# Attention into a token and channel mixer on one core: five small moves in the start-up, and a third output tile

## The chip, the cores and the metric

The kernel runs on one core of a Trainium2 chip. The metric is the device time of one execution in microseconds (us). Three runs of the kernel before gave 394.48, 394.86 and 395.20 us, with a median of 394.86 us.

The engines are named as in the profile: PE is the matrix engine (PEld its weight loads), DVE the vector engine, ACT the scalar engine, POOL the GpSimd engine, SP the engine that only issues transfers here. A line number such as L301 is a line of the kernel before.

## What is computed

Cosine attention over 8 batches, 12 heads, 448 positions and 64 elements per head, and behind it a mixer over tokens and channels:

```python
q_n = q / (norm(q) + 1e-06);  k_n = k / (norm(k) + 1e-06)      # over the 64 elements
attn = softmax(q_n @ k_n.T / tau)                               # tau = 0.1
x = (attn @ v), heads side by side                              # 8 x 448 x 768
h = relu(x.T @ w_tok1) @ w_tok2                                 # 448 -> 256 -> 448, over tokens
u = x + h.T
out = u + relu(u @ w_ch1) @ w_ch2                               # 768 -> 1536 -> 768, over channels
```

Inputs, weights and output are 32-bit floats.

## The kernel before, in words

**Units of work.** Two heads of one batch make a pair; there are 48 pairs, six to a batch, and three pairs make a "half" (half 0 is pairs 0 to 2, half 1 is pairs 3 to 5, and so on). A sequence of 448 positions is held as three chunks of 128 ("main") and a rest of 64 ("x" in the names: `xq`, `xk`, `xv`, `sqx`).

**What a pair goes through.** Squares of q and k (`squares`, `squares_x`, line 178 on ACT, line 180 on DVE or POOL), their sums by DVE (`sums`, `sums_x`, lines 193 and 197), reciprocal norms by four short ACT operations (`rnorms`, lines 201 to 204), scaling of k and q by these norms (`scaled` line 211, `scaled_x` lines 217 and 222, mostly POOL), transposes on PE into the PSUM tile `pst` (`tpose`, lines 243 to 248), a DVE copy of it to `qk` (`qk_copy`, line 261), three main score products into `psS` and their exponentials on ACT (`score`, lines 301 and 302), one product for the rest (`score_x`, lines 308 and 309), the product with the values into `psO` (`pv`, lines 320 and 322), and the division on DVE (`rec` line 326, `x` line 327). From pair 15 on the transposes are done by the DMA engines instead.

**The mixer.** `m_tok1` multiplies by `w1t` into `psR` (line 341) and DVE takes the positive part to `r` (line 344). `m_tok2` multiplies by `w2t` into `psU` (line 361), adds x through the identity (line 366), and DVE casts the sum to `ut` (line 368). Six pairs complete a batch; then `m_ch1` (`psG`, lines 389 and 391) and `m_ch2` (`psF`, line 404) do the channel part, in units that are fed in between the steps of later pairs. The result is added to the transposed u by DVE into an output tile `ost` (line 407), which a DMA on SP's queue sends out (lines 414 to 417). Each `ost` tile is filled by two such additions; the pool `outp` holds two tiles.

**Order of the work.** The order on every engine is that of the program text; nothing reorders it. After a start-up written out by hand, a loop over slots i = 0 to 49 issues the steps; tables such as `sq_at`, `sum_at`, `rn_at`, `sc_at` and `cast_at` say in which slot a pair's squares, sums, norms, scaling and value casts stand. Each engine works through its own list in order, and waits at the head of it. PSUM tiles come from two rings: `ps2` with three places for `psS`, `psX`, `psO` and `psR`, and `ps` with two for `pst`, `psG`, `psF` and (for the first two batches) `psU`.

**What the change and the steps below touch.**
- `weights_tok` (lines 140 to 144) issues three DMAs on POOL's queue, which convert from 32 to 16 bits on the way: the main part of `w1t`, its rest of 64 rows, and `w2n`, the second token weight as it lies in memory. It stands in the start-up behind `score_x(0)`.
- `place_w2` (lines 147 and 149) and `place_w2_odd` (line 152) copy `w2n` on DVE into the order that `m_tok2` wants: `w2t` has columns XR to S for the main positions, and the 64 rest positions both behind them (line 149, columns S to S+64) and ahead of them (line 152, columns 0 to 64), since even batches read columns 64 to 512 and odd ones 0 to 448. `place_w2` stands at the end of slot 2, `place_w2_odd` at the end of slot 3.
- `cast_v` (line 166) casts a half's values to `vt`; for half 1 it stands in slot 3, ahead of the `m_tok2` of pair 0. `cast_vx` (line 172, POOL) does the rest rows.
- The squares of pair 3 and those of the rest rows of half 1 stand in slot 0, both q and k on ACT.

Of the kernel before, what the change touches and what calls it, by code (L numbers as in the profile page):

```python
# [22 lines left out]
def kernel(  # L23
# [12 lines left out]
    nc = tc.nc  # L36

    B, H, S, E = q.shape
# [5 lines left out]
    NC = 3  # L44
    SM = P * NC
# [93 lines left out]

    def weights_tok():  # L140
        nc.gpsimd.dma_start(out=w1t[:, 0:NC, :], in_=moe_w_tok1[0:SM].rearrange("(p c) t -> p c t", c=NC))
        nc.gpsimd.dma_start(out=w1t[0:XR, NC, :], in_=moe_w_tok1[SM:S])
        w2n.append(mix.tile([P, TT, S], FP16, name="w2n", tag="gt16", bufs=1))
        nc.gpsimd.dma_start(out=w2n[0][:], in_=moe_w_tok2.rearrange("(tt p) s -> p tt s", p=P))

    def place_w2():
        nc.vector.tensor_copy(out=w2t[:, :, XR:S].rearrange("t a (c p) -> t a c p", c=NC),
                              in_=w2n[0][:, :, 0:SM].rearrange("t a (p c) -> t a c p", c=NC))
        nc.vector.tensor_copy(out=w2t[:, :, S:S + XR], in_=w2n[0][:, :, SM:S])  # L149

    def place_w2_odd():
        nc.vector.tensor_copy(out=w2t[:, :, 0:XR], in_=w2n[0][:, :, SM:S])

# [301 lines left out]
    early_sq = {3: 0, 4: 1, 5: 1, 6: 3, 7: 4, 8: 5, 9: 5, 10: 6, 11: 7, 12: 8, 13: 9, 14: 9, 15: 10, 16: 11, 17: 11}  # L455
    sq_slot = {p: early_sq.get(p, p - 6) for p in range(3, NP_ALL)}
    sq_at = at(sq_slot)
    sum_at = at({p: s + 1 for p, s in sq_slot.items() if p < 8 or p >= 18})

    rn_at = {}  # L460
    for n in range(1, NHALF):
        for c0, c1 in ((0, 21), (21, 45)) if n < 4 else ((0, 45),):
            s = 1 + sq_slot[3 * n + (0 if c1 == 21 else 2)]
            rn_at.setdefault(s, []).append((n, c0, c1))
# [47 lines left out]
    with tc.manual_schedule():  # L512
# [75 lines left out]
        score_x(0)  # L588
        weights_tok()
        cast_vx(0)  # L590
        cast_v(0)
        scaled(2, nc.gpsimd)
        for i in range(NP_ALL + 2):
# [30 lines left out]
            def next_sq(ps):  # L624
                for p in ps:
                    norm_begin(p, nc.scalar if p < 18 else nc.gpsimd, nc.scalar if p == 3 else nc.vector if p in (10, 11, 12, 15) else nc.gpsimd)

# [144 lines left out]
```

## Time and profile before

| | |
|---|---|
| three runs | 394.48, 394.86, 395.20 us |
| the profiled execution | 394.72 us |
| its span, first to last instruction | 392.9 us |
| PE busy | 378.7 us (96%) |
| ACT, POOL, DVE busy | 225.8, 209.6, 193.5 us |
| bytes moved by DMA | 67.51 MB, 172 GB/s in the mean |

Where PE was busy, by stretches of the span (us):

| stretch | length | PE busy |
|---|---|---|
| 0 to 10 | 10 | 8.39 |
| 10 to 30 (slots 0 to 3) | 20 | 14.32 |
| 30 to 45 | 15 | 13.35 |
| 45 to 90 | 45 | 44.31 |
| 90 to 100 | 10 | 8.79 |
| 100 to 380 | 280 | 279.86 |
| 380 to 392.9 | 12.9 | 9.70 |

Engine rows of the timeline read "start, length, engine, line, operation, output <- inputs, shapes, count", and in brackets the idle time ahead of it with what ended it. A length includes the tail of an operation, which overlaps the next one; the spacing of the starts is the time that an operation costs its engine when several stand in a row. The list of waits reads "who waited <- for whom: total us, times, longest us". The chain of waits follows the last instruction back through whatever released each step, and reads "start, length, engine, line".

### The profile page before, as it was taken

How to read it: one execution, taken by the hardware profiler on the slowest of the kernel's cores; microseconds unless marked ns; L12 is line 12 of the kernel's file. 1: busy time of each engine (PE TensorE's matmuls, PEld its weight loads, DVE VectorE, ACT ScalarE, POOL GpSimd, SP SyncE). 2: the span in 40 equal slices, each digit the busy share in tenths (PEclk: the TensorE clock that was granted, in tenths of full speed). 3: DMA queues.
4: the chain of work that ended last, by engine and by line, in shares of the span. 5: the costliest groups of instructions: out<-in, count | busy, mean ns of one | idle time of the engine just before them, and what ended most of it. 6: DMA issues, size and time to landing. Idle time of an engine off the chain costs nothing.

```text
span 392.9 us, 9076 instructions
## 1 busy us (share of the span) xinstructions
PE 378.7 (96%) x3658; PEld 228.5 (58%) x3658; DVE 193.5 (49%) x368; ACT 225.8 (57%) x411; POOL 209.6 (53%) x306
## 2 busy tenths in 40 slices
PE   8678999998999999999999999999999999999996
PEld 3346555665565656566556566566566566565554
DVE  5688758865344554545524645345534342333022
ACT  5998698843774639573676446673775536511400
POOL 4978486789267584868572947659561700000000
PEclk9899999999999999999999999999999999999999
DMA  7999999969968987999989899999982452013013
GB/s 203 276 238 253 246 236 215 227 138 264 209 131 190 202 183 179 222 183 208 205 199 198 175 245 216 166 189 182 242 142 56 123 123 68 16 57 102 5 40 120
DMA packets 137514, 67.51 MB, mean 172 GB/s; under 512 B 93248, under 2 KB 134016, under 8 KB 137472
## 3 DMA queue, kind: packets, MB, share of 16 engines
q1 hardware_dynamic: 133296, 61.36, 71.4%
q0 software_dynamic: 3632, 5.18, 7.4%
q8 instruction: 28, 0.46, 0.5%
q10 hardware_dynamic: 544, 0.39, 0.3%
q14 instruction: 14, 0.11, 0.1%
HBM read 43.38 MB, written 11.01 MB: 138 GB/s over the span
## 4 chain that ended last, share of the span: by engine, by line
PE 86%; ACT 6%; DVE 3%; DMA 2%; SPq 1%; issue 1%; ACTq 0%; DVEq 0%
PE psF L404 28%; PE psG L389 27%; PE psO L320 9%; PE psS L301 7%; PE psR L341 5%; PE psU L361 4%; ACT pt L302 3%; PE psO L322 3%; PE psX L308 2%; DMA out_dram<-ost 1%; DMA km<-in_k_dram 1%; PE psU L366 1%; PE pst L243 1%; ACT sq L178 1%; DVE ost L407 1%
## 5 line engine op out<-in xcount | busy, mean ns | idle before, releaser
L302 ACT ACTIVATE pt<-psS 128x896 f16<-128x896 f32 x141 | 119.0, 921 | 65.8 <-PE psS L301 65.5
L389 PE MATMUL psG<-ut,wc1t 128*128 128x448 f16 x576 | 119.5, 353 | 0.2
L404 PE MATMUL psF<-wc2t,gt 128*128 128x384 f16 (+2 forms) x684 | 117.3, 324 | 1.2 <-DVE ost L407 1.1
L391 ACT ACTIVATE gt<-psG 128x448 f16<-128x448 f32 x96 | 51.1, 557 | 73.2 <-PE psG L389 73.2
L404 PEld LDWEIGHTS <-gt 128*128 128x128 f16 x684 | 64.5, 98 | 48.4 <-issue 8.1
L389 PEld LDWEIGHTS <-wc1t 128*128 128x128 f16 x576 | 53.2, 98 | 52.5 <-issue 8.7
L211 POOL TENSOR_TENSOR kq<-km,rn 128x384 f16<-128x384 f32 x47 | 39.4, 837 | 80.9 <-ACT rn L204 80.7
L407 DVE TENSOR_TENSOR ost<-psF,ur 128x384 f32<-128x384 f32 (+2 forms) x57 | 31.4, 550 | 90.0 <-PE psF L404 86.6
L320 PEld LDWEIGHTS <-pt 128*128 128x128 f16 x1152 | 50.1, 97 | 8.4 <-issue 2.4
L320 PE MATMUL psO<-vt,pt 128*128 128x65 f16 x1152 | 52.4, 193 | 1.2 <-ACT pt L302 0.8
L326 DVE RECIPROCAL rec<-psO 128x8 f32<-128x8 f32 x48 | 9.9, 207 | 80.9 <-PE psO L322 80.9
L193 DVE TENSOR_REDUCE ssq<-sq 128x12 f32<-128x768 f32 (+1 forms) x49 | 45.1, 929 | 5.3 <-ACT sq L178 3.7
L322 PE MATMUL psO<-vx,pt 128*128 128x130 f16 x192 | 41.8, 218 | 0.0
L180 POOL TENSOR_TENSOR sq<-km 128x384 f32<-128x384 f32 x42 | 34.5, 823 | 13.2 <-DMA km<-in_k_dram 13.0
L211 POOL TENSOR_TENSOR kq<-qm,rn 128x384 f16<-128x384 f32 x47 | 39.5, 841 | 0.0
L301 PE MATMUL psS<-qk 64*128 64x448 f16 x282 | 36.1, 357 | 2.0 <-DVE qk L261 0.9
L327 DVE TENSOR_TENSOR x<-psO,rec 128x512 f16<-128x512 f32 x48 | 33.2, 691 | 1.7
L341 PE MATMUL psR<-x,w1t 128*128 128x128 f16 x384 | 29.2, 219 | 0.1
L309 ACT ACTIVATE pt<-psX 128x448 f16<-128x448 f32 x48 | 27.1, 564 | 3.3 <-PE psX L308 2.3
L361 PE MATMUL psU<-w2t,r 128*128 128x448 f16 x96 | 25.9, 353 | 1.5 <-DVE w2t L149 1.1
L180 POOL TENSOR_TENSOR sq<-qm 128x384 f32<-128x384 f32 x30 | 24.7, 822 | 2.4 <-DVE ssq L193 1.6
L341 PEld LDWEIGHTS <-w1t 128*128 128x128 f16 x384 | 23.8, 97 | 2.1 <-issue 0.3
(76 smaller groups left out, 320.8 us busy)
## 6 DMA issues: line engine op xcount, KB each, us to landing
vm<-in_v_dram SPq DMA_DIRECT2D x16, 576.0 KB, 5.0
out_dram<-ost SPq DMA_DIRECT2D x23, 384.0 KB, 3.1
qm<-in_q_dram SPq DMA_DIRECT2D x14, 576.0 KB, 5.1
km<-in_k_dram SPq DMA_DIRECT2D x14, 576.0 KB, 5.6
wc1t<-in_moe_w_ch_dram POOLq DMA_DIRECT2D x2, 1152.0 KB, 13.8
wc2t<-in_moe_w_ch_dram POOLq DMA_DIRECT2D x2, 1152.0 KB, 12.6
out_dram<-ost SPq DMA_DIRECT2D x9, 192.0 KB, 2.7
xq<-in_q_dram SPq DMA_DIRECT2D x7, 192.0 KB, 5.2
```

Source lines behind the costliest of these rows:

```text
L180: eng.tensor_tensor(out=out, in0=src, in1=src, op=ALU.mult)
L193: nc.vector.tensor_reduce(out=ssqs[p // HP % 3][:, lo + 6 * a0:lo + 6 * a1], in_=sq[p][:, a0:a1].rearrange("p a g e -> p (a g) e"), axis=A ...
L211: eng.tensor_tensor(out=kqs[n % 2][:, j, a, 0:NC, :].rearrange("p c (g e) -> p g c e", g=2), in0=src, in1=_bcast_free(rn, E), op=ALU.mult)
L301: nc.tensor.matmul(psS[:, g, 0:S], qk[r, P * c:P * (c + 1)], qk[r, 512:512 + S], start=True, stop=True)
L302: nc.scalar.activation(out=pt[:, 2 * S * c:2 * S * (c + 1)].rearrange("p (g s) -> p g s", g=2), in_=psS[:, :, 0:S], func=AF.Exp, scale=inv ...
L320: nc.tensor.matmul(psO[:, m, E1 * g:E1 * (g + 1)], pt[:, at:at + P], vt[:, 2 * j + g, c, 0:E1], start=(g == 0 and c == 0), stop=False)
L322: nc.tensor.matmul(psO[:, m, 0:2 * E1], pt[:, PX + P * m:PX + P * (m + 1)], vx[:, j, 0:2 * E1], start=False, stop=True)
L341: nc.tensor.matmul(psR[:, tt, :], w1t[:, m, tt * P:(tt + 1) * P], xs[p][:, m, :], start=(m == 0), stop=(m == NC))
L361: nc.tensor.matmul(psU, rs[p][:, tt, :], w2t[:, tt, lo:lo + S], start=(tt == 0), stop=by_dma and tt == TT - 1)
L389: nc.tensor.matmul(psG[:], wc1t[:, dt, ct * P:(ct + 1) * P], ut[:, dt, sp], start=(dt == 0), stop=(dt == DT - 1))
L391: nc.scalar.activation(out=gt[:, ct, sp], in_=psG[:], func=AF.Relu)
L404: nc.tensor.matmul(psF[:, 0:w], gt[:, ct, lo:lo + P], wc2t[:, ct, P * i0:P * i1], start=(ct == 0), stop=(ct == CT - 1))
```

## The change

- The pool of output tiles goes from two to three.
- `weights_tok` is split. The DMA of `w2n` and that of the main part of `w1t` are issued on POOL's queue ahead of POOL's scaling of pair 1; only the rest of `w1t` stays where all three were.
- `place_w2` keeps the main columns alone and stands in slot 1, behind the sums of that slot. The two copies of the rest columns become `place_w2_x(lo)`: columns S on at the end of slot 2, columns 0 on at the end of slot 3.
- The squares of pair 3 and of the rest rows of half 1 move from slot 0 to the end of the start-up, ahead of POOL's scaling of pair 2; q stays on ACT (the rest rows first), k goes to POOL.
- `cast_v(1)` moves from the middle of slot 3 to its end, behind the copy to columns 0 to 64. On DVE it so moves from ahead of the cast of pair 0's u to ahead of the sums of pair 6.

```diff
-    outp = ctx.enter_context(tc.tile_pool(name="outp", bufs=2))
+    outp = ctx.enter_context(tc.tile_pool(name="outp", bufs=3))
...
-    def weights_tok():
-        nc.gpsimd.dma_start(out=w1t[:, 0:NC, :], in_=moe_w_tok1[0:SM].rearrange("(p c) t -> p c t", c=NC))
-        nc.gpsimd.dma_start(out=w1t[0:XR, NC, :], in_=moe_w_tok1[SM:S])
+    def weights_tok1(x):
+        if x:
+            nc.gpsimd.dma_start(out=w1t[0:XR, NC, :], in_=moe_w_tok1[SM:S])
+        else:
+            nc.gpsimd.dma_start(out=w1t[:, 0:NC, :], in_=moe_w_tok1[0:SM].rearrange("(p c) t -> p c t", c=NC))
+
+    def weights_tok2():
         w2n.append(mix.tile([P, TT, S], FP16, name="w2n", tag="gt16", bufs=1))
         nc.gpsimd.dma_start(out=w2n[0][:], in_=moe_w_tok2.rearrange("(tt p) s -> p tt s", p=P))
...
     def place_w2():
         nc.vector.tensor_copy(out=w2t[:, :, XR:S].rearrange("t a (c p) -> t a c p", c=NC),
                               in_=w2n[0][:, :, 0:SM].rearrange("t a (p c) -> t a c p", c=NC))
-        nc.vector.tensor_copy(out=w2t[:, :, S:S + XR], in_=w2n[0][:, :, SM:S])
-
-    def place_w2_odd():
-        nc.vector.tensor_copy(out=w2t[:, :, 0:XR], in_=w2n[0][:, :, SM:S])
+
+    def place_w2_x(lo):
+        nc.vector.tensor_copy(out=w2t[:, :, lo:lo + XR], in_=w2n[0][:, :, SM:S])
...
-    early_sq = {3: 0, 4: 1, 5: 1, 6: 3, ...}
-    sq_slot = {p: early_sq.get(p, p - 6) for p in range(3, NP_ALL)}
+    early_sq = {4: 1, 5: 1, 6: 3, ...}
+    sq_slot = {p: early_sq.get(p, p - 6) for p in range(4, NP_ALL)}
...
-    cast_at = at({n: {1: 3, 2: 6}.get(n, 3 * n - 2) for n in range(1, NHALF)})
+    cast_at = at({n: {2: 6}.get(n, 3 * n - 2) for n in range(2, NHALF)})
...
         squares_x(0, nc.scalar, nc.gpsimd)
+        weights_tok2()
+        weights_tok1(0)
         rnorms(0, 21, 33)
         scaled(1, nc.gpsimd)
...
         score_x(0)
-        weights_tok()
+        weights_tok1(1)
         cast_vx(0)
         cast_v(0)
+        squares_x(1, nc.scalar, nc.gpsimd)
+        squares(3, nc.scalar, nc.gpsimd)
         scaled(2, nc.gpsimd)
...
             for p in sum_at.get(i, ()):
                 norm_sums(p)
+            if i == 1:
+                place_w2()
...
             if i == 2:
-                place_w2()
+                place_w2_x(S)
             if i == 3:
-                place_w2_odd()
+                place_w2_x(0)
+                cast_v(1)
```

The slots of the sums and norms of pair 3 stay as they were, and no instruction of PE or SP moves.

More of the change, by code (lines that the diff above doesn't have):

```diff
@@ L454 @@
     FIRST = NPAIR
-    early_sq = {3: 0, 4: 1, 5: 1, 6: 3, 7: 4, 8: 5, 9: 5, 10: 6, 11: 7, 12: 8, 13: 9, 14: 9, 15: 10, 16: 11, 17: 11}
-    sq_slot = {p: early_sq.get(p, p - 6) for p in range(3, NP_ALL)}
+    early_sq = {4: 1, 5: 1, 6: 3, 7: 4, 8: 5, 9: 5, 10: 6, 11: 7, 12: 8, 13: 9, 14: 9, 15: 10, 16: 11, 17: 11}
+    sq_slot = {p: early_sq.get(p, p - 6) for p in range(4, NP_ALL)}
     sq_at = at(sq_slot)
-    sum_at = at({p: s + 1 for p, s in sq_slot.items() if p < 8 or p >= 18})
+    sum_at = at({p: s + 1 for p, s in ({3: 0} | sq_slot).items() if p < 8 or p >= 18})
     rn_at = {}
@@ L462 @@
         for c0, c1 in ((0, 21), (21, 45)) if n < 4 else ((0, 45),):
-            s = 1 + sq_slot[3 * n + (0 if c1 == 21 else 2)]
+            s = 1 + ({3: 0} | sq_slot)[3 * n + (0 if c1 == 21 else 2)]
             rn_at.setdefault(s, []).append((n, c0, c1))
@@ L625, in next_sq @@
                 for p in ps:
-                    norm_begin(p, nc.scalar if p < 18 else nc.gpsimd, nc.scalar if p == 3 else nc.vector if p in (10, 11, 12, 15) else nc.gpsimd)
+                    norm_begin(p, nc.scalar if p < 18 else nc.gpsimd, nc.vector if p in (10, 11, 12, 15) else nc.gpsimd)
             if i == FIRST:
```

## The prediction

> **What bounds the kernel now.** I read first where PE is idle, stage by stage. From 100 to 380 us it is busy for 279.86 of 280 us: nothing the change touches can shorten that, but what is gained ahead of it arrives at the end whole. Idle time lies at 10 to 45 us (7.3 us) and at 90 to 100 us (1.2 us). The list of PE's waits shows which of it the change can reach:
>
> ```profile
> PE psU L361 <- DVE w2t L149: 1.1, 1, 1.1
> PE psF L404 <- DVE ost L407: 1.1, 1, 1.1
> ```
>
> Two single waits of 1.1 us. The chain of waits says what stands behind the first:
>
> ```profile
> 24.81 0.56 DVE qk L261
> 25.37 0.33 DVE r L344
> 25.70 1.00 DVE w2t L147
> 26.70 0.75 DVE w2t L149
> 27.45 0.04 issue
> 27.50 0.54 PE psU L361 x2
> ```
>
> The reader sees 1.75 us of placing w2, and PE starting pair 0's psU when it ends. Behind the second, from the same view:
>
> ```profile
> 88.70 0.57 DVE ost L407
> 89.27 0.10 SPq L380
> 89.37 0.05 issue
> 89.41 0.02 SPq L414
> 89.43 0.03 issue
> 89.46 4.61 DMA out_dram<-ost
> 94.07 0.03 issue
> 94.10 0.02 DVEq L407
> 94.12 0.04 issue
> 94.17 0.57 DVE ost L407
> 94.73 0.04 issue
> 94.78 2.12 PE psF L404 x12
> ```
>
> The third output tile is the first one over again; its DMA is issued at 89.46 and lands at 94.07, DVE stands for 3.4 us, and PE for 1.13 of them. Last, the engine rows between 15 and 45 us: ACT has no gaps from 15 to 41 us but 0.87 and 0.45 at 30, so a cut on PE or DVE there is worth only what reaches the next exponential.
>
> **Part 1, third output tile: -1.13 us.** The tile at 94.17 no longer waits for a DMA. Its psF had ended at about 91.4; DVE then does that addition, the qk copy (PE's transposes ended at 92.1), rec, x and r without a stop. PE's psR ends at 93.64 and psF follows at once: 94.78 - 93.64 = 1.14, of which the list charges 1.13. What is late next? psU of that slot needs r; r would end near 94.5 and psF at 95.6, so no new wait. The next tile of the ring is used at about 148 us. Bounds: 0 (PE stopped by something else there) to -1.13.
>
> **Part 2, squares of pair 3 and rest rows: -0.15 us.** ACT's rows start at 15.47, 15.88, 16.30, 16.71 and the first exponential of pair 1 at 17.00: the two k operations go (0.41 + 0.29), so ACT is free at 16.30. But psS starts at 16.40, and an exponential starts 0.40 us behind its psS (30.67 to 31.07, 43.03 to 43.44); the granted clock is 0.50 between 14 and 17 us, so I put it at 16.85. POOL takes 0.50 (rest rows) and 0.82 more, but gives up two DMA issues there (0.74, 0.73): it reaches the scaling of pair 2 at 12.95 + 0.92 + 0.74 + 0.46 + 0.79 = 15.9 (16.15 before). Its next wait is for norms at 20.58, and it was through at 19.3, so 1.3 us are spare. DVE's sums of pair 3 wait for ACT's q square (16.3) or POOL's k square (15.9), 16.45 before. Bounds: 0 to -0.7.
>
> **Part 3, weights fetched early: 0 us.** POOL issues them between its rest-row square (ends 7.56) and the scaling of pair 1, which waits for norms until 9.10. 0.73 + 0.74 fit in 1.54 us; if the issues take 0.92 each, as one did, pair 1's scaling is 0.3 late, needed only by transposes at 14.38 (it ended at 10.72). No instruction is queued on SP behind them. Transfers: POOL's queue moved 5.18 MB in 7.4% of 392.9 us, 29.1 us of all 16 engines; 416 KB are 2.4 us of that. The DMA engines are at 0.54 and 0.44 at 9 to 11 us, so perhaps 0.9 us goes into that hole and 1.5 us competes with half 0's values, issued at 8.38, landing at 13.1. At 14.6 (13.1 + 1.5) their cast (0.67) still ends before the qk copy of pair 1 at 15.54: cover until a landing at 14.85. The rest rows of the values land at 13.75, perhaps 15.2; POOL would then finish pair 3's k square at 17.0, and DVE's sums start 0.6 us later than before; the exponentials of pair 2 can bear that, since ACT, not DVE, holds them (psS at 20.70, ACT free at 21.73, 0.6 us spare). Every us beyond these covers is a us. Bounds: -0.1 to +0.6.
>
> [...] The landings of before speak rather for SP's loads going first (these weights took 6.3 and 7.3 us beside them); then the values stay at 13.1. Both lie ahead of 14.85, and the sum is the same.
>
> **Part 4, w2 in slot 1, cast behind U: -0.45 us.** The main copy (1.0) stands in slot 1 between the sums (end 17.9 by part 2) and rec of pair 0, which waits for PE until 19.14: 1.0 in some 1.1 us, with the same 0.6 us spare behind. If a copy meets POOL's work, both stretch: POOL's L211 took 1.14 beside it at 26.25 against 0.83.
>
> [...]
>
> Slot 3, with the -0.15 carried: DVE's r ends at 25.55, the rest copy takes 0.40 to 0.75, PE ends psS at 26.2, so psU starts near 26.2 instead of 27.50. Next late is POOL: pst of pair 4 needs the scaling that began at 25.46; now 25.31 + 0.79 + 0.83 = 26.93. pst at 26.95 against 28.07: **-1.12**, and psO, x and the exponentials of pair 4 with it (x ends 29.62, exponentials 29.95). But from x of pair 2 (30.74) to the copy of pair 5's qk (34.35) DVE's rows stand without a gap: r 0.33, rest copy 0.40, sums 0.86 and 0.66, ut 0.53, rec 0.22, x 0.61. The moved cast now stands in that row, behind U and ahead of the sums: **+0.67** (47.70 to 48.37). So the qk copy, the psS behind it (35.06) and the exponentials of pair 5 (35.46) come 1.12 - 0.67 = 0.45 us earlier, and ACT is not the later one (its norms wait for those sums). Queued behind the cast: everything just named; who waits: ACT for the sums, PE for qk. From there the chain (ACT to 38.85, PE, DVE, PE from 43.70) is passed on as it is. Part 2's -0.15 is contained in this. Bounds: -1.12 (the cast hidden) to +0.10 (cast 0.91 as at 27.36, scaling 0.31 longer as at 26.25: -1.12 + 0.91 + 0.31). I take -0.45, since the cast of 0.67 is the one that met no POOL work, and POOL waits for its norms just there.
>
> **The sum**, against the profiled execution: 394.72 - 0.45 - 1.13 = 393.14. That execution is 0.14 under the median of the three runs (394.86), within their spread, so I say **393.1**. All bounds at their best: 394.72 - 1.12 - 1.13 = 392.5; at their worst: 394.72 + 0.1 = 394.8.
>
> **Rivals.**
> - *The start gives nothing* (0.18): the cast, late value loads or POOL beside the copies take the 0.45 back; only the tile counts, 394.72 - 1.13 = 393.6. For it: DVE has no gap from 28.3 to 33.5 us. Against: 1.75 us really leave DVE ahead of psU.
> - *The output tile gives nothing* (0.10): SP issues in order and lies seven us behind there (the first tile was full at 82.3, sent at 89.46); what comes 1.1 us earlier on PE may wait for transposed qk or u later. 394.72 - 0.45 = 394.3. Against: PE waits for no DMA after 100 us.
> - *The cast is hidden* (0.09), because psU comes still earlier: 392.5.
> - *Slower: DVE stands at place_w2 in slot 1* (0.06). It is queued ahead of rec, x and the qk copy of pair 2, and waits for w2n, issued at 7.6. That landed in 7.3 us before; a landing at 14.9 is 3 us early. From a landing at 18.75 each us costs one (1.0 copy, 0.6 spare); from 20.3, 12.7 us after the issue, it outweighs the 1.58 gained. Rows of such length exist (wc1t 13.9, km 20.1 us, both in a crowded queue). At 22 us: 3.25 - 1.58 gives 396.4.
>
> **How the numbers follow.** My forecast, 393.1, gets 0.57. Range 392.4 to 394.5: it holds the forecast, the two rivals short of one part, and the best case at its edge; it leaves out the slower one and the worst ends, under 2 in 10. A measurement of this kernel tells about 0.2% (0.8 us, so 394.07) from no change. Faster by over that: forecast, first and third rival, 0.84; within it: the second rival, 0.10; slower: 0.06.
>
> **What would show it.** PE's list of waits without both lines; DVE's ost at 94 us without a DMA; the w2t copy on DVE between sums and rec near 18 us, w2n landed by 15; exponentials of pair 5 near 35.0, with the vt cast between the rest copy and the sums; psF without a gap near 93. Wrong if half 0's value cast or pair 1's qk copy starts after 15.6, if DVE waits for w2n, or if PE shows new gaps beyond 100 us.

## The result, and the profile after

The changed kernel takes **396.0 us** (five runs, 395.96 to 396.10) beside 394.91 us for the kernel before (five runs, 394.48 to 395.66): a ratio of 1.0025, with a 95% interval of 1.0011 to 1.004. It is slower by a quarter of a per cent, about 1 us. The prediction said 393.1 us. The profiled execution of after took 395.96 us, its span is 394.2 us; before it was 394.72 and 392.9.

In the kernel after, every line number below L137 is a few higher: L361 is now L364, L404 is L407, and so on. Its list of PE's waits begins so ("who waited <- for whom: total us, times, longest us"):

```profile
PE psS L304 <- DVE qk L264: 2.6, 2, 1.5
PE pst L250 <- DVE kq L225: 2.5, 1, 2.5
```

Both lines that the change was to remove, psU behind `w2t` and psF behind `ost`, are gone. In their place stand others: before, psS waited 0.9 us in all for qk, and pst 1.8 us for kq. Busy time by stretches tells the same from the other end (columns: length, busy time and count of PE, PEld, DVE, ACT and POOL, granted clock of PE, share of the DMA engines, GB/s):

```profile
10.00:45.00 35.00, 27.67 (x366) 18.08 (x366) 26.54 (x49) 29.89 (x64) 28.43 (x42) 0.95 1.12 257
```

That is the row of before; these are the rows of after:

```profile
10.00:45.00 35.00, 26.17 (x342) 17.53 (x338) 26.05 (x45) 27.64 (x59) 27.19 (x41) 0.90 1.12 252
```

```profile
90.00:100.00 10.00, 9.93 (x95) 6.02 (x94) 6.34 (x11) 3.08 (x4) 9.72 (x15) 1.00 1.17 239
100.00:380.00 280.00, 279.85 (x2647) 167.76 (x2647) 119.84 (x236) 153.42 (x260) 137.86 (x193) 1.00 0.75 156
```

From 90 to 100 us PE is busy for 9.93 us where it was 8.79: the third output tile gave its 1.14 us. From 100 to 380 us nothing has changed (279.85 us of PE in both). From 10 to 45 us PE gets through 342 products instead of 366, at a mean clock of 0.90 instead of 0.95. The loss is in the start-up, and the chain of waits leads through it ("start, length, what"):

```profile
8.75 6.94 DMA xv<-in_v_dram
15.69 0.05 issue
15.74 0.22 POOL vx L175
...
16.48 0.36 POOL vx L175
16.84 0.07 issue
16.91 0.51 POOL sqx L183
17.42 0.79 POOL sq L183
18.21 0.02 issue
18.24 0.95 DVE ssq L196
19.19 0.66 DVE ssq L200
19.85 1.13 DVE w2t L151
20.98 0.13 DVE rec L329
21.11 0.02 issue
21.13 0.45 DVE x L330
21.58 0.16 issue
21.74 0.66 DVE qk L264
22.40 0.05 issue
22.44 0.38 PE psS L304 x2
```

Read from the top: the rest rows of half 0's values land at 15.69. POOL stands for them, and behind its cast of them are queued the squares of pair 3 that the change gave to POOL. DVE's sums wait for those until 18.24. Behind the sums stands the new copy of w2, and behind the copy rec, x and the qk copy that PE needs. Every instruction in this chain was either added here, moved here, or put behind one that was.

To compare kernels I use six marks in each trace: the start of DVE's scaling of pair 0's k, and the starts of the first exponentials of pairs 1 to 5. Behind the exponential of pair 5 all kernels run alike for the next 8.0 us, and then PE is the bound. From that exponential to the end of the span it is 357.4 us in the kernel before, and 356.1 to 356.5 us in all the others, which have the third output tile. The spacings, in us, worked out from the timelines:

| kernel | to pair 1 | 1 to 2 | 2 to 3 | 3 to 4 | 4 to 5 | sum |
|---|---|---|---|---|---|---|
| before | 9.23 | 4.73 | 4.14 | 5.20 | 4.39 | 27.69 |
| after | 10.02 | 5.32 | 5.68 | 4.21 | 5.26 | 30.49 |
| difference | +0.79 | +0.59 | +1.54 | -0.99 | +0.87 | +2.80 |

Behind the last mark after needs 356.2 us where before needs 357.4, 1.24 less (the output tile), and its first mark lies 0.26 us earlier (7.51 instead of 7.77). That makes 2.80 - 1.24 - 0.26 = +1.30, and the spans differ by 1.3.

### The profile page after: what moved, and what is told of

Its sections match the earlier page's. It is cut to its first block, busy times and chain, and to the rows that moved or that the text cites. A ratio compares the mean times of both kernels' runs of the same rounds, so it can differ in the third digit from the quotient of the medians.

```text
span 394.2 us, 9074 instructions
## 1 busy us (share of the span) xinstructions
PE 378.1 (96%) x3658; PEld 229.1 (58%) x3658; DVE 194.6 (49%) x368; ACT 225.4 (57%) x409; POOL 210.4 (53%) x308
## 4 chain that ended last, share of the span: by engine, by line
PE 88%; DVE 4%; DMA 3%; ACT 3%; SPq 1%; issue 1%; POOL 0%; ACTq 0%; POOLq 0%; DVEq 0%
PE psF L407 28%; PE psG L392 27%; PE psO L323 9%; PE psS L304 7%; PE psR L344 5%; PE psU L364 4%; PE psO L325 3%; PE psX L311 2%; DMA xv<-in_v_dram 2%; ACT pt L305 1%; DMA km<-in_k_dram 1%; PE pst L246 1%; PE psU L369 1%; DVE x L330 1%; DVE ssq L196 0%
## 5 line engine op out<-in xcount | busy, mean ns | idle before, releaser
L407 PE MATMUL psF<-wc2t,gt 128*128 128x384 f16 (+2 forms) x684 | 117.3, 323 | 0.1
L407 PEld LDWEIGHTS <-gt 128*128 128x128 f16 x684 | 64.5, 98 | 47.1 <-issue 6.8
L183 POOL TENSOR_TENSOR sq<-km 128x384 f32<-128x384 f32 x43 | 35.6, 830 | 11.7 <-DMA km<-in_k_dram 11.5
L330 DVE TENSOR_TENSOR x<-psO,rec 128x512 f16<-128x512 f32 x48 | 33.2, 691 | 1.7
L364 PE MATMUL psU<-w2t,r 128*128 128x448 f16 x96 | 25.9, 353 | 0.3 <-DVE ut L371 0.3
## 6 DMA issues: line engine op xcount, KB each, us to landing
wc2t<-in_moe_w_ch_dram POOLq DMA_DIRECT2D x2, 1152.0 KB, 13.1
```

The costliest lines, as they stand in the source:

```text
L183: eng.tensor_tensor(out=out, in0=src, in1=src, op=ALU.mult)
L364: nc.tensor.matmul(psU, rs[p][:, tt, :], w2t[:, tt, lo:lo + S], start=(tt == 0), stop=by_dma and tt == TT - 1)
L407: nc.tensor.matmul(psF[:, 0:w], gt[:, ct, lo:lo + P], wc2t[:, ct, P * i0:P * i1], start=(ct == 0), stop=(ct == CT - 1))
```

## The experiments

My theory from this profile: the tile gives what it was priced at, and four costs take more than it gives: the cast in its new place, the early transfers, POOL's queue ahead of pair 3's squares, and TensorE's clock, which is granted at 0.50 for two stretches of 3.4 us where before had one. The rival: one of them does all the harm, and undoing it gives the forecast. A second rival: the clock alone does it.

The table has all runs, with n in brackets. Rows that follow each other with the same time of before were measured together, on one chip. "Sum" is that of the six marks.

| kernel | median us | before us | ratio, 95% | sum |
|---|---|---|---|---|
| tile_alone | 393.70 (4) | 395.18 (25) | 0.9948, 0.993 to 0.9965 | 28.08 |
| rest_cast_behind | 395.60 (10) | 395.18 | 1.0001, 0.9987 to 1.0016 | 29.32 |
| fetch_late | 394.77 (10) | 395.18 | 0.998, 0.9965 to 0.9994 | 29.49 |
| fill_slot2 | 396.27 (10) | 395.18 | 1.0021, 0.9998 to 1.0044 | 30.49 |
| cast_ahead | 394.57 (10) | 395.15 (31) | 0.9972, 0.9951 to 0.9993 | 28.04 |
| w1_late | 394.69 (10) | 395.15 | 0.9985, 0.9963 to 1.0007 | 29.14 |
| squares_act | 395.37 (10) | 395.15 | 0.9997, 0.9976 to 1.0018 | 29.57 |
| w2_alone | 393.81 (10) | 395.15 | 0.9954, 0.9935 to 0.9973 | 28.59 |
| tile_fill | 393.70 (10) | 395.14 (28) | 0.9967, 0.995 to 0.9984 | 27.64 |
| w2_fill | 393.27 (7) | 395.14 | 0.9951, 0.9935 to 0.9966 | 27.54 |
| after_fill | 395.30 (10) | 395.14 | 1.0005, 0.9992 to 1.0018 | 29.45 |
| repaired_fill | 393.75 (10) | 395.14 | 0.9959, 0.9946 to 0.9972 | 28.15 |
| cast_alone | 395.38 (10) | 395.28 (25) | 1.0001, 0.9991 to 1.0011 | 30.09 |
| fetch_alone | 394.62 (10) | 395.28 | 0.9981, 0.9968 to 0.9995 | 28.11 |
| best | 393.82 (10) | 395.28 | 0.9956, 0.9941 to 0.9972 | 28.19 |

### The tile, POOL's queue, the early fetch, the clock

**tile_alone**: the kernel before with the third output tile and nothing else.

```diff
-    outp = ctx.enter_context(tc.tile_pool(name="outp", bufs=2))
+    outp = ctx.enter_context(tc.tile_pool(name="outp", bufs=3))
```

> The kernel before with three output tiles and nothing else. If the gain of the third tile stands by itself: PE's wait of 1.1 us at psF goes, nothing new appears behind it, 393.8 us (before 394.9). If it is given back later: no gap of PE at 94 us, but one elsewhere, 394.9.

Measured 393.70 against 395.18, 1.5 us less (by the ratio's interval 1.4 to 2.8). It is the only large gain in the change, and it was priced at 1.13. PE no longer waits for `ost`, and behind pair 5 the profile is 1.2 us shorter; what makes the medians differ by a little more is not shown.

**rest_cast_behind**: the kernel after, with POOL's cast of the rest rows moved behind the squares of the rest rows and of pair 3.

```diff
-        cast_vx(0)
         cast_v(0)
         squares_x(1, nc.scalar, nc.gpsimd)
         squares(3, nc.scalar, nc.gpsimd)
+        cast_vx(0)
```

> The changed kernel with one move on POOL: the cast of half 0's rest rows of v goes behind the two k squares. Queue theory (POOL stands at that cast until the load lands at 15.7, and the squares, DVE's sums, the w2 copy, rec and pair 2's qk copy stand behind it): sums of pair 3 near 16.6 instead of 18.24, rec of pair 0 near 19.7 instead of 20.90, no half clock at 24 to 27 us, 393.3 to 394.6 us (changed kernel 396.0). Port theory (the time is lost before, in DVE's scaling of the rest rows, 2.03 against 0.89 us): that row stays at 2.0 and the time at 395.7 to 396.0.

POOL's rows in this kernel show that the squares no longer stand behind the wait:

```profile
14.10 0.82 POOL L183 TENSOR_TENSOR sq<-km 128x384 f32<-128x384 f32 x1
15.54 0.75 POOL L175 CAST vx<-xv 64x192 f16<-64x192 f32 x2 [0.61 <-DMA xv<-in_v_dram]
```

The square of pair 3's k starts at 14.10 instead of 17.38, the sums at 17.06 instead of 18.24, and the step from pair 1 to pair 2 takes 4.80 instead of 5.32 (before: 4.73). So the place of that wait in POOL's queue cost the 0.5 us of that step. The rest stays: the way to pair 1 takes 10.14 and DVE's scaling of the rest rows 1.82, pair 4 to 5 takes 6.01, and the ratio is 1.0001. The time is far above the 393.3 to 394.6 that I expected of this theory, and just under the range of the other.

**fetch_late**: the kernel after, with all token weights fetched where they were before, and the main copy of w2 at the end of slot 2 again.

```diff
-        weights_tok2()
-        weights_tok1(0)
         rnorms(0, 21, 33)
...
+        weights_tok1(0)
         weights_tok1(1)
+        weights_tok2()
         cast_vx(0)
...
-            if i == 1:
-                place_w2()
...
             if i == 2:
+                place_w2()
                 place_w2_x(S)
```

> The changed kernel with the early fetch undone: all three weight loads where they were, the main copy of w2 at the end of slot 2 again, ahead of the rest copy; tile, squares and value cast as changed. Queue theory: half 0's values land near 13.1 and 13.8 again, the start is as before up to pair 2, the copies cost PE their 1.1 us at psU again, and with the third tile it is 393.6 to 394.3 us. Rival (the moved cast, 1.35 us in a row of DVE without a gap, or the squares on POOL cost the time): the loss stays, 395.3 to 396.0.

The way to pair 1 is 9.31, as before; psU waits for w2t for 1.14 us again; and still pair 4 to 5 takes 6.12. The value cast of half 0 starts at 13.51, without a wait. Pair 1 to 2 takes 4.73, as before, although the squares are on POOL here: their place costs nothing when the values come in time. The median lies between my two ranges, and the two causes were not rivals: the early fetch costs, and the moved cast costs too.

**fill_slot2**: the kernel after, with nine filler products instead of two ahead of pair 2's score. (The kernel before has such fillers at the head of slots 1 to 3: products with the identity into the tile that the score then overwrites. They only keep PE active.)

```diff
-                score(i, 0, 2 if i < 4 else 0)
+                score(i, 0, 9 if i == 2 else 2 if i < 4 else 0)
```

> The changed kernel with nine fillers instead of two ahead of pair 2's scores (seven more products whose result is overwritten), in the 1.54 us in which PE waits for pair 2's qk copy; nothing else moves. If the half clock at 24.4 to 27.2 us is a price of its own: the clock stays at 1.00, psR and the fillers of slot 3 take 0.6 instead of 1.0 us, the exponentials of pair 3 start near 27.5 instead of 28.53, 394.8 to 395.2 us. If only the late qk copy counts: 396.0.

There is no stretch of half clock at 24 us, and pair 2 to 3 takes 4.15 instead of 5.68; but the first stretch holds from 14.6 to 21.5 us here, 6.8 us at 0.50 as in both stretches of after together. Pair 1 to 2 takes 6.16 and pair 4 to 5 6.01, and the median is 396.27, above both ranges. One place of fillers moved the time about and gained nothing.

### The others undone, one at a time

**cast_ahead**: the kernel after with half 1's value cast where it was before, ahead of U in slot 3.

```diff
-    cast_at = at({n: {2: 6}.get(n, 3 * n - 2) for n in range(2, NHALF)})
+    cast_at = at({n: {1: 3, 2: 6}.get(n, 3 * n - 2) for n in range(1, NHALF)})
...
                 place_w2_x(0)
-                cast_v(1)
```

> The changed kernel with the cast of half 1's values back in slot 3 ahead of pair 0's U. Cast theory (behind U the cast stands in a row of DVE without a gap, beside POOL's work, and takes 1.35 us of it, where ahead of U it fills the 1.33 us in which DVE waits for psU): DVE's sums of pair 6 near 32.7 instead of 34.0, exponentials of pair 5 five to nine tenths earlier than 38.0, 394.8 to 395.4 us (changed kernel 396.0). If only the early fetch costs: 395.9 to 396.0.

394.57 us: the largest repair by a single edit. Pair 4 to 5 takes 4.33 and pair 3 to 4 4.22, so here the gain on psU is kept whole: pair 2 to 5 takes 12.69 where before has 13.73. The cast takes 1.43 here too (27.73 to 29.09), but in time in which DVE had nothing else to do.

**w1_late**: the kernel after with the main part of w1 fetched at its old place, w2n still early.

```diff
         weights_tok2()
-        weights_tok1(0)
         rnorms(0, 21, 33)
...
+        weights_tok1(0)
         weights_tok1(1)
         cast_vx(0)
```

> The changed kernel with the main part of w1 fetched where it was, so that only w2n goes early (224 of 416 KB, and one issue of 0.89 us instead of two on POOL). Queue and port theory: POOL is done with its issue before the norms come, DVE's scaling of the rest rows takes 0.9 instead of 2.03 us, half 0's values land near 14.5 and 14.9 instead of 15.4 and 15.7, the exponentials of pair 1 start 0.7 us earlier and those of pair 2 one to two; 393.8 to 395.0 us. If w2n alone is what displaces the values, or the squares on POOL cost by themselves: 395.5 to 396.0.

The way to pair 1 is 9.11, half 0's value cast starts at 14.87 instead of 15.46, and DVE's scaling of rest rows takes 0.90 again instead of 2.03. 394.69 us, as expected. But the exponentials of pair 2 come only 0.34 us earlier, not one to two: pair 1 to 2 takes 5.66 here, with the half clock from 15.8 to 22.6 us.

**squares_act**: the kernel after with the squares of pair 3 and of half 1's rest rows back on ACT in slot 0.

```diff
-        squares_x(1, nc.scalar, nc.gpsimd)
-        squares(3, nc.scalar, nc.gpsimd)
...
-    early_sq = {4: 1, 5: 1, 6: 3, ...}
+    early_sq = {3: 0, 4: 1, 5: 1, 6: 3, ...}
...
-                    norm_begin(p, nc.scalar if p < 18 else nc.gpsimd, nc.vector if p in (10, 11, 12, 15) else nc.gpsimd)
+                    norm_begin(p, nc.scalar if p < 18 else nc.gpsimd, nc.scalar if p == 3 else nc.vector if p in (10, 11, 12, 15) else nc.gpsimd)
```

> The changed kernel with the squares of pair 3 and the rest rows back in slot 0, all on ACT. If pair 3's sums are late because POOL stands at the cast of the rest rows of v with the k square behind it: the sums start near 17.6 instead of 18.24, rec of pair 0 near 20.2 instead of 20.90, the start itself (exponentials of pair 1) gains nothing or loses 0.2, 394.8 to 395.6 us. If POOL's place in line does not count, ACT's 0.7 us more make it 396.0 to 396.5.

The sums of pair 3 start at 16.74 instead of 18.24. But in this run the half clock held from 15 to 21.7 us, twice as long, and pair 1 to 2 took 5.32 all the same: the gain can't be read from this run. 395.37 us, in the expected range.

**w2_alone**: the kernel before with three output tiles, w2n alone fetched early, its main copy in slot 1 and the two rest copies in slots 2 and 3.

```diff
+        weights_tok2()
         rnorms(0, 21, 33)
...
+            if i == 1:
+                place_w2()
...
             if i == 2:
-                place_w2()
+                place_w2_x(S)
             if i == 3:
-                place_w2_odd()
+                place_w2_x(0)
```

> The kernel before with three output tiles, w2n alone fetched ahead of pair 1's scaling, its main copy in slot 1 and the rest copies in slots 2 and 3; squares on ACT, value cast ahead of U, w1 as before. If the copy's 1.1 us ahead of psU is worth what I said once nothing is paid for it: 392.6 to 393.3 us, that is 0.4 to 1.1 under the third tile alone (393.7). If the place in slot 1, or the early transfer by itself, costs as much as the copy: 393.6 to 394.3.

393.81 us, no less than the tile alone, as my second range had it. PE waits for w2t no more, but pair 3 to 4 takes 4.72 and 4 to 5 4.76, where cast_ahead has 4.22 and 4.33. The timelines say why. First POOL's scaling and DVE's cast in w2_alone:

```profile
26.33 0.83 POOL L212 TENSOR_TENSOR kq<-km,rn 128x384 f16<-128x384 f32 x1 [2.09 <-ACT rn L205]
27.12 1.45 POOL L212 TENSOR_TENSOR kq<-qm,rn 128x384 f16<-128x384 f32 x1
```

```profile
27.14 0.75 DVE L167 CAST vt<-vm 128x1152 f16<-128x1152 f32 x1
```

and then the same two in cast_ahead:

```profile
27.72 0.83 POOL L214 TENSOR_TENSOR kq<-qm,rn 128x384 f16<-128x384 f32 x1
```

```profile
27.73 1.43 DVE L169 CAST vt<-vm 128x1152 f16<-128x1152 f32 x1
```

The two start within 0.02 us of each other, POOL's row first in both. In one kernel DVE takes 0.75 and POOL 1.45, in the other POOL 0.83 and DVE 1.43. Where POOL's is the long one, the scaling of pair 4 comes late, and the time won at psU is lost there. w2_fill, repaired_fill and best below go the way of w2_alone (0.75 for DVE, 1.44 to 1.45 for POOL), with POOL's start 0.01 us ahead as in cast_ahead; so the recorded starts do not tell which of the two will be the long one.

### Without the half clock

Four kernels with more fillers, in three places: 8 ahead of pair 0's last transposes, 3 ahead of its rest scores, and more at the head of slots 1 and 2 (the numbers in the diff are those of **after_fill**; at the heads of slots 1 and 2 **tile_fill** has 2 and 3, **w2_fill** and **repaired_fill** have 6 and 4).

```diff
         score_main0(2)
+        busy(w, 8)
         tpose_x(0, pst)
...
+        busy(w, 3)
         score_rest0()
...
-                score(i, 0, 2 if i < 4 else 0)
+                score(i, 0, {1: 7, 2: 8, 3: 2}.get(i, 0))
```

tile_fill is tile_alone with them, w2_fill is w2_alone with them, after_fill is the kernel after with them, and repaired_fill is the kernel after with the edits of cast_ahead and w1_late, and with them.

> The kernel before with three output tiles and fillers (products whose result is overwritten) in PE's start-up gaps: 8 ahead of the rest transposes of pair 0, 3 ahead of its rest scores, 3 instead of 2 ahead of pair 2's scores. Clock theory (an idle stretch of PE between 10.5 and 14 us costs one or two stretches of 3.4 us at half clock behind it): the granted clock stays at 1.00 from 14 to 26 us, mean 0.998 or more (0.991 to 0.996 without), 393.0 to 393.5 us against 393.7. If ACT and DVE hold the start anyway: 393.6 to 393.8, and less spread of the runs.

> The kernel with the third tile, w2n alone fetched early and its copy in slot 1 (393.8 us without fillers), with fillers in PE's start-up gaps: 8, 3, then 6 and 4 instead of 2 ahead of the scores of pairs 1 and 2. If the 6.8 us at half clock ate what the copy saved at psU: clock 1.00 throughout, exponentials of pair 2 near 21.9 instead of 22.6, 392.4 to 393.2 us. If half 0's later values did: 393.6 to 393.9.

> The changed kernel with fillers in PE's start-up gaps: 8, 3, then 7 and 8 instead of 2 ahead of the scores of pairs 1 and 2. Nothing else moves, so half 0's values land as late and POOL stands as long. Clock theory: no half clock, 394.6 to 395.3 us (changed kernel 396.0). If the clock only fills waits that are there anyway: 395.8 to 396.1.

> The changed kernel with the three repairs together: value cast of half 1 ahead of U, main part of w1 fetched where it was, fillers (8, 3, 6 and 4). The single repairs gave 394.6 and 394.7 us (changed kernel 396.0). If the costs are separate and add: 392.4 to 393.3 us, below the third tile alone (393.7). If they overlap: 393.5 to 394.3.

The fillers do hold the clock: its mean is 1.00 in all ten runs of after_fill, and 0.987 to 0.990 in the five of after. With that, after_fill takes 395.30 us, 0.7 us less than after (not measured side by side; by their ratios to before it is 0.8), and it is still no faster than the kernel before. So the clock accounts for part of the loss, not for all of it, and the second rival falls. In tile_fill the fillers gained nothing in the median (393.70, as tile_alone, the second of my ranges), although its clock is 0.995 to 1.00. **w2_fill**, 393.27 us, is the fastest kernel run: 1.9 us under before (by the interval 1.3 to 2.6), some 2.7 us under after, which was not measured beside it; it lies just above the range that I had hoped for. repaired_fill has 393.75: with the cast back and w1 late, what is left of the change gives nothing beyond the tile.

### The two suspects alone

**cast_alone**: tile_alone with one edit, half 1's cast behind U.

```diff
-    cast_at = at({n: {1: 3, 2: 6}.get(n, 3 * n - 2) for n in range(1, NHALF)})
+    cast_at = at({n: {2: 6}.get(n, 3 * n - 2) for n in range(2, NHALF)})
...
             if i == 3:
                 place_w2_odd()
+                cast_v(1)
```

> The kernel before with three output tiles (393.7 us) and half 1's value cast behind U, nothing else. If the cast beside POOL takes 1.35 us in DVE's row without a gap and the rest copy 0.8: exponentials of pair 5 start 6.0 us behind those of pair 4 instead of 4.4, and 394.6 to 395.4 us. If it costs the bare 0.67 that I priced: 5.1 us, 394.2 to 394.5.

395.38 us: that one edit eats the whole gain of the tile. Pair 4 to 5 takes 6.12, tile_alone has 4.33 and tile_fill 4.40: 1.7 to 1.8 us. DVE's rows in cast_alone, from the r of pair 1:

```profile
31.28 0.42 DVE L344 TENSOR_SCALAR r<-psR 128x256 f16<-128x256 f32 x1
31.61 0.85 DVE L152 COPY w2t<-w2n 128x128 f16<-128x128 f16 x1
32.38 1.43 DVE L166 CAST vt<-vm 128x1152 f16<-128x1152 f32 x1
33.73 0.94 DVE L193 TENSOR_REDUCE ssq<-sq 128x12 f32<-128x768 f32 x1
```

and beside them POOL's:

```profile
30.80 0.82 POOL L211 TENSOR_TENSOR kq<-km,rn 128x384 f16<-128x384 f32 x1
31.59 0.82 POOL L211 TENSOR_TENSOR kq<-qm,rn 128x384 f16<-128x384 f32 x1
32.37 0.82 POOL L180 TENSOR_TENSOR sq<-km 128x384 f32<-128x384 f32 x1
```

POOL's row from 29.55 to 33.2 has no gap. The copy starts 0.02 behind one POOL operation and the cast 0.01 behind another; copy and cast end only after those (32.46 and 33.81, against 32.41 and 33.19), while POOL keeps its 0.82 throughout. From r to the sums DVE needs 33.73 - 31.28 = 2.45 us; the kernel before needs 31.47 - 30.74 = 0.73. The difference is 1.72.

**fetch_alone**: tile_alone with w2n and w1's main part issued early, and nothing else moved.

```diff
+        weights_tok2()
+        weights_tok1(0)
         rnorms(0, 21, 33)
...
-        weights_tok()
+        weights_tok1(1)
         cast_vx(0)
```

> The kernel before with three output tiles (393.7 us) and w2n and the main part of w1 fetched ahead of pair 1's scaling; the copies, squares and cast stay where they were. If the early transfer costs by itself (DVE's scaling of the rest rows loses to POOL, half 0's values land at 15.4, more half clock): exponentials of pair 1 start 9.9 to 10.1 us behind DVE's scaling of pair 0 instead of 9.2, 394.1 to 395.0 us. If its cost comes only with the squares queued on POOL: 393.6 to 393.9.

394.62 us against 395.28, a gain of 0.7 where the tile alone gave 1.5: the early transfer costs about 0.8 by the medians of two kernels that were not run side by side, and 0.4 by the way to pair 1 (9.58 against 9.20). I had expected a way of 9.9 to 10.1; DVE's scaling of the rest rows takes 0.91 here, not the 2.03 of after. DVE's cast of half 0's values now waits for its load:

```profile
15.42 0.76 DVE L170 CAST vt<-vm 128x1152 f16<-128x1152 f32 x1 [1.58 <-DMA vm<-in_v_dram]
```

**best**: repaired_fill with the edit of rest_cast_behind as well.

> The changed kernel with four repairs: value cast of half 1 ahead of U, main part of w1 fetched where it was, POOL's cast of half 0's rest rows behind the squares of pair 3, fillers (8, 3, 6 and 4). If pair 3's sums no longer wait behind that cast: exponentials of pair 2 start 4.7 to 4.8 us behind those of pair 1 instead of 5.6, and 392.4 to 393.1 us, below the version with w2n alone and fillers (393.3). If another wait takes its place (POOL's squares beside DVE's value cast): 393.2 to 393.7.

393.82 us, above both ranges. Pair 1 to 2 takes 4.73, as hoped (5.61 in repaired_fill; both at full clock), but the way to pair 1 takes 9.85 instead of 8.90, since half 0's value cast starts at 15.64 in this run. It gains nothing on w2_fill.

## Why the prediction was wrong

**Part 1, the output tile: right.** Priced at -1.13; the gap at 94 us is gone, PE is busy for 9.93 of the 10 us there, and behind pair 5 every kernel with the tile is 0.9 to 1.3 us shorter. tile_alone is 1.5 us faster, 1.4 to 2.8 by its interval.

**Part 4, the moved cast: the step that failed, and the largest.** I wrote "+0.67 (47.70 to 48.37)", with 0.91 as the bound, "since the cast of 0.67 is the one that met no POOL work, and POOL waits for its norms just there". POOL does not wait for its norms there: in the timeline of before it works without a gap from 29.42 to 33.0, and the cast's new place is 31.5. Those rows were at hand:

```profile
31.46 0.82 POOL L211 TENSOR_TENSOR kq<-qm,rn 128x384 f16<-128x384 f32 x1
32.25 0.82 POOL L180 TENSOR_TENSOR sq<-km 128x384 f32<-128x384 f32 x1
```

In the kernel after the cast met them:

```profile
32.38 0.35 DVE L155 COPY w2t<-w2n 128x128 f16<-128x128 f16 x1
32.65 1.43 DVE L169 CAST vt<-vm 128x1152 f16<-128x1152 f32 x1
34.00 0.94 DVE L196 TENSOR_REDUCE ssq<-sq 128x12 f32<-128x768 f32 x1
```

1.35 from start to start, twice 0.67; in cast_alone, with the rest copy at 0.85 as well, the whole move costs 1.72. The other term of that part was right where it could be seen by itself: in cast_ahead, pair 3 to 5 takes 4.22 + 4.33 = 8.55 against 5.20 + 4.39 = 9.59 before, -1.04 where I had -1.12. So part 4 is -1.04 + 1.72 = +0.68, not -0.45; after_fill, at full clock throughout, has both in one kernel and +0.66 over pair 2 to 5. That gain has a condition that I had only as a bound: in w2_alone, w2_fill, repaired_fill and best, where POOL's scaling was the long one (1.44 to 1.45 for 0.83), the same two steps took 9.47 to 9.49, and -0.1 is left of it.

The 1.75 us of copies that the gain came from were no fixed price either. In tile_alone, where they still stand in slot 2, they cost DVE 0.47 and 0.25 us from start to start instead of 1.01 and 0.73; POOL's cast beside them takes 1.62, and PE does not wait for `w2t`. That kernel has 4.22 and 4.33 for pair 3 to 5 too, behind a pair 2 to 3 of 5.61 with half clock in it. So the two steps alone would not show the gain; what shows it is pair 2 to 5, 12.69 in cast_ahead against 13.73 in before and in tile_fill.

The rows of before already had DVE's copies at about twice their length or more (1.09 and 0.81, against 0.55 and 0.33 in tile_alone), and a cast and an operation of POOL lengthened (0.93 for 0.75, 1.14 for 0.83). I had weighed such a meeting at the copy in slot 1, where there was time to spare, and not at the cast in slot 3, where there was none.

**Part 3, the early fetch: "0 us" failed twice.** First on POOL. I had the two issues as 0.73 + 0.74, and said that if they took more, the scaling of pair 1 "is 0.3 late, needed only at 14.38". POOL's rows of after:

```profile
7.57 0.89 POOL L148 DMA_DIRECT2D w2n<-in_moe_w_tok_dram  x1
8.46 0.58 POOL L144 DMA_DIRECT2D w1t<-in_moe_w_tok_dram  x1
9.05 0.84 POOL L214 TENSOR_TENSOR kq<-km,rn 128x384 f16<-128x384 f32 x1
9.85 0.83 POOL L214 TENSOR_TENSOR kq<-qm,rn 128x384 f16<-128x384 f32 x1
10.64 0.82 POOL L183 TENSOR_TENSOR sq<-km 128x384 f32<-128x384 f32 x1
```

The first norms were ready at about 8.8, and the scaling starts at 9.05 behind the issues. It is hardly late, and its own result is in time; but its neighbour is not. DVE's next row:

```profile
10.50 2.03 DVE L220 TENSOR_TENSOR kq<-xq,rn 64x128 f16<-64x128 f32 x1 [0.67 <-ACT rn L207]
```

Before, this operation took 0.89 and started 0.08 us behind POOL's square (10.76 and 10.68). Now it starts 0.14 ahead of it and takes 2.03. Over all 17 traces: in 14 kernels DVE starts behind POOL's square and takes 0.89 to 0.96; in three (after, after_fill, rest_cast_behind) it starts 0.03 to 0.21 ahead of it and takes 1.82 to 2.03. Four other kernels issue both fetches early and do not have it (DVE starts 0.01 to 0.06 behind there), so the early issues bring it about only in some executions. The rest scaling of k follows, and PE's wait for it grows from 1.8 to 2.5. In after this, and not the late values, set the way to pair 1: PE works without a gap from the rest scores of pair 0 at 14.29 (13.84 before), at half clock as before, and comes to psS of pair 1 without having waited for it:

```profile
16.93 1.10 PE L304 MATMUL psS<-qk 64*128 64x448 f16 x6
```

The qk copy that it needs, behind the late value cast, starts at 16.14 and takes 0.65; it was in time. rest_cast_behind says the same: its value cast met no wait, and its way to pair 1 is 10.14.

Second, the value loads. I had half 0's at 14.6 at the latest, and its rest rows at 15.2. They landed at 15.4 and 15.7:

```profile
15.46 0.76 DVE L169 CAST vt<-vm 128x1152 f16<-128x1152 f32 x1 [1.23 <-DMA vm<-in_v_dram]
```

```profile
15.74 1.09 POOL L175 CAST vx<-xv 64x192 f16<-64x192 f32 x2 [2.28 <-DMA xv<-in_v_dram]
```

The prediction had named this sign itself: wrong if pair 1's qk copy starts after 15.6; it starts at 16.14. Where the scaling took 0.91 to 0.96, these loads set the way to pair 1: in cast_ahead and fetch_alone PE waits 0.41 and 0.20 us at psS for the copy behind them, and the way is 9.85 and 9.58. Either cause is enough by itself. The load of 576 KB took 7.3 us instead of 4.7, that of the rest rows 6.9. I had put the values at 14.6 if 1.5 us of the weights compete with them, and at 13.1 if SP's loads go first. They did not stay at 13.1: w2n, issued at 7.57, landed at 12.8, 5.2 us behind its issue (7.3 in before), and half 0's values landed behind it, 2.3 us later than in before. That is more than the 1.5 us that I had reckoned for 416 KB (the hole at 9 to 11 us was filled: 1.06 and 0.82 where it had 0.54 and 0.44); and in rest_cast_behind, with the same two fetches, the load took 6.1 us, and the value cast started at 14.26 without a wait. The size is not settled by my sum, and how the transfers shared the DMA engines, no run shows.

**Part 2, the squares on POOL: the spare time was not there.** I counted 1.3 us to spare on POOL, behind a cast of the rest rows that I let run through at 0.74. POOL stood there for 2.28 us, with the square of pair 3 behind it; I had put that square's end at 15.9, 17.0 at worst; it was 18.2. I had seen the late landing and the queue, and had said that the exponentials of pair 2 "can bear that". They could not: the rows behind the sums (w2 copy 1.13, rec, x, qk) are the chain shown above, and pair 1 to 2 takes 0.59 longer. rest_cast_behind gives that back (4.80 against 4.73 before), and so does the same move from repaired_fill to best (5.61 to 4.73). The step has another cause in other runs: cast_alone and w2_alone keep the squares on ACT and have 5.44 and 5.47. In w2_alone the clock is at half until 22.2 us; in cast_alone PE's two fillers at 20.91 take 0.96 us from start to start, and those at 25.49 take 0.53. And fetch_late, with the squares on POOL and the values in time, has 4.73. So the squares on POOL cost only what the late values make of them.

**What had no term at all: the clock.** The stop of PE at 22.44 (1.54 us) is followed by a stretch at half clock:

```profile
23.00:24.00 1.00, 0.37 (x8) 0.28 (x7) 1.00 (x2) 1.00 (x2) 1.00 (x3) 1.00 1.16 233
24.00:25.00 1.00, 1.00 (x28) 1.00 (x25) 0.11 (x1) 1.00 (x2) 0.93 (x3) 0.76 1.07 284
25.00:26.00 1.00, 1.00 (x10) 0.78 (x8) 0.71 (x2) 0.94 (x4) 0.07 (x1) 0.50 1.27 222
26.00:27.00 1.00, 1.00 (x11) 0.74 (x9) 0.65 (x2) 0.84 (x3) 0.42 (x1) 0.50 1.18 184
27.00:28.00 1.00, 1.00 (x7) 0.41 (x4) 0.69 (x3) 0.00 (x0) 1.00 (x2) 0.54 1.07 276
```

From the rows at 24, 25, 26 and 27 us it is (0.48 + 1 + 1 + 0.92) = 3.4 us long at 0.50. (A row of clock c has the share 2 x (1 - c) of it, taking 0.50 inside the stretch and 1.00 outside, as the rows at 23, 25 and 26 us have it.) psR takes 1.04 in it instead of 0.62, and pair 2 to 3 takes 5.68 instead of 4.14. In the profiled execution of before there was one such stretch, at 14 to 17 us, also 3.4 us long; in that of after there are two. By after_fill they cost 0.7 us together. But so much half clock is not peculiar to the change: of the 109 runs of before that were measured beside the experiments, 82 have a mean clock of 0.987 to 0.991, like profiles with 6.8 us or more at half clock, and 27 have 0.995 or 0.996, like the profiled one; their medians are 395.29 and 394.91 us. Of the five runs of after two have 0.990 and three 0.987.

**The sum.** Against the profiled executions, by the marks: first mark -0.26, way to pair 1 +0.79 (DVE's scaling of the rest rows, 2.03 for 0.89, here), pair 1 to 2 +0.59 (POOL's queue behind the late values), pair 2 to 5 +1.42, tile -1.24; together +1.30. The +1.42 splits by after_fill, whose clock is 1.00 throughout: pair 2 to 5 takes 14.39 there, 13.73 before and 15.15 in after, so +0.66 belongs to cast and psU and +0.76 to the clock. This split holds for these executions. Most runs of before have a mean clock like that of profiles with 6.8 us or more at half, so it does not say how much of the loss in the medians is the clock's.

**The rivals.** "The start gives nothing" named the three right causes, "the cast, late value loads or POOL beside the copies", and stopped them at zero, as if they could only use up the 0.45. The moved cast was larger than that by itself (1.72), and the late loads about as large (0.4 in fetch_alone). For this rival I had written that DVE has no gap from 28.3 to 33.5 us; it has one of 0.43, at 29.45, ahead of the cast's new place. The slower rival, DVE standing for w2n, did not happen: w2n landed at 12.8, and the copy of it stood at 19.77, 7 us later. The bounds of the parts were taken one at a time, each with its own cover; but the covers were one another: DVE's 0.6 us spare was used in part 3 and again in part 4.

**One cause or several.** Not one. cast_ahead, w1_late, fetch_late and after_fill each lie 0.7 to 1.4 us under the 396.0 of after, rest_cast_behind and squares_act 0.4 and 0.6 (after was measured before them, not beside them). They do not add up: cast_ahead, w1_late and after_fill alone make 3.4, and repaired_fill, which has all three repairs, lies 2.25 under after. Part of that is that one wait covers another; part is that in repaired_fill POOL's scaling is the long one (1.45), with 9.49 for pair 3 to 5. The runs do not separate the two.

**Left open.** Why the cast of half 0's values starts anywhere between 14.26 and 16.38 in kernels that fetch early. Which of DVE's cast and POOL's scaling is the long one when both start within 0.02 us. Why DVE's 64-row operation takes 1.82 to 2.03 us, and not 0.89 to 0.96, when it starts ahead of POOL's. The kernel after with two output tiles was not run, so the loss of the other four parts together, 2.3 us by the difference to tile_alone (396.0 and 393.7), is taken from runs that were not made side by side. And the share of half clock differs between runs of one kernel: squares_act has 395.0 to 395.6 at a mean clock of 0.991 and 395.8 to 396.5 at 0.987.

## What to carry to other kernels

Price a moved DVE operation by the rows of POOL at its new place, not by its own row at the old one: where POOL worked without a gap, the cast took 1.43 for 0.75 (after, cast_alone). Price the other outcome too, in which POOL's operation is the long one, here 1.45 for 0.83 (w2_alone), and see what hangs on it. The early fetch was paid for here by the loads beside it (7.3 us for half 0's values instead of 4.7) and by every instruction queued behind a wait for them, so write down the whole queue of an in-order engine behind its first wait before calling its time spare. And count a cover once: if two edits are hidden by the same idle 0.6 us, one of them is not hidden.

## What the runs showed of the hardware

- DVE's 128x1152 cast and a 128x384 operation of POOL that started within 0.02 us of each other took 0.75 and 1.44 to 1.45 (w2_alone, w2_fill, repaired_fill, best), or 1.43 and 0.82 to 0.83 (after, cast_ahead, cast_alone). Both outcomes occurred with POOL's recorded start 0.01 us ahead of DVE's (best and after).
- A 64x128 DVE operation took 0.89 to 0.96 when it started 0.01 to 0.08 us behind POOL's square (14 kernels), and 1.82 to 2.03 when it started 0.03 to 0.21 us ahead of it (after, after_fill, rest_cast_behind). The square took 0.81 to 0.83 in all of them.
- POOL's DMA issues took between 0.54 and 0.92 us for the same three transfers, by their place: w2n 0.89 when issued early, 0.72 to 0.75 at its old place; the rest of w1 0.54 (w2_alone) to 0.92 (before).
- The 576 KB load of half 0's values took 4.6 to 5.5 us from issue to landing where the token weights were issued at their old place (before, tile_alone, tile_fill, fetch_late, cast_alone), and 6.1 to 7.4 in the other kernels, where w2n's issue started ahead of it.
- The granted clock of PE in after was 0.50 for 3.4 us behind a stretch in which PE had not been idle throughout: from 21 to 24 us it was busy for 0.00, 0.56 and 0.37 of each us, 0.31 in the mean. In before 0.66, 0.36 and 0.56 from 20 to 23 us were not followed by such a stretch. Others were longer: 6.8 us in one piece in fill_slot2, w1_late and squares_act, 10.2 in cast_ahead. What sets their start and length, no run shows.
